# Top-k attention and a SwiGLU block: where the epsilon is added, when the reciprocal runs, and the order of the first loads

## The chip, the core and the metric

The kernel runs on one core of a Trainium2 chip. A core has five engines that run side by side, each with its own instruction queue in program order: TensorE (PE in the profile, with its weight loads as PEld), VectorE (DVE), ScalarE (ACT), GpSimd (POOL) and SyncE (SP), which here only issues DMA transfers. They meet through semaphores. The metric is the device time of the whole kernel in microseconds, the median of several runs.

## What is computed

```python
# q, k, v: (8 batches, 8 heads, 576 rows, 64)
scores = scale * np.matmul(q, k.transpose(0, 1, 3, 2))
kth = np.partition(scores, -top_k, axis=-1)[..., -top_k:-top_k + 1]      # top_k = 32
scores = np.where(scores >= kth, scores, -1000000000.0)
attn = np.exp(scores - np.max(scores, axis=-1, keepdims=True))
attn = attn / (np.sum(attn, axis=-1, keepdims=True) + 1e-09)
x = np.matmul(attn, v)                      # then to (4608 tokens, 512)
g = x @ w_gate                              # (512, 1536)
out = (g * (1.0 / (1.0 + np.exp(-g))) * (x @ w_val)) @ w_out             # (1536, 512)
```

All is float32. The 1e-09 is the epsilon of this document.

## The kernel before

**Units.** Attention is cut into 160 units: for each of 8 batches, five tiles of query rows (four of 128 rows, one of the 64 rows left over), and for each tile four pairs of heads. `units` (line 273) lists them in this order, so units 0 to 19 are batch 0. A unit of a full tile has two heads per instruction pair, one of the last tile has both heads stacked in one (units 16 to 19, 36 to 39 and so on). In the loop over `n` (line 833) the selection of unit `n`, the softmax of unit `n - 1`, the transposes of unit `n - 2` and the product with V of units `n - 4` and `n - 3` stand side by side.

**Selection on VectorE.** `select` (line 318) finds the 32 largest of 576 scores in four rounds: MAX8 finds eight, MATCH_REPLACE8 strikes them out. With two heads this makes seven pairs of instructions: MAX8, MATCH, MAX8, MATCH, MAX8, MATCH, MAX8. The helper `dve(k)` (line 840) emits `k` of these pairs, and after some of them a step of the rounding of the weights (`rounding`), unless it is told `beside=False`.

**Softmax.** `shift` (line 340) puts the bias of the exponential on GpSimd. `weigh` (line 350) runs on ScalarE: a Prelu that masks, then an Exp that also sums its row into `tot`. `normalize` (line 368) adds the epsilon to `tot` and takes the reciprocal, both on VectorE, and after a `yield` multiplies `e` by it: on GpSimd for both heads of units 0 to 11 (line 380), from unit 12 on the first head on ScalarE (line 378) and the second on GpSimd. In the loop the line `run(norm)` (line 890) stands between the fifth pair of the selection (`dve(1)`, line 888) and the last two (`dve(2, beside=False)`, line 891). `turn` (line 384) transposes `e` on TensorE, and ScalarE copies the result out of PSUM.

**Loads and preparation.** `load` (line 215) fetches K and Q of one pair of heads: for K and then for Q, two transfers of the 512 main rows and one of the last 64 rows. All go through SP's queue, except two of pair 0, which ScalarE issues. `prep` (line 250) transposes them on TensorE in three steps, each with a PSUM bank from `ps_t` (5 banks) and copies by ScalarE: K's main rows, the last rows of both, Q's main rows, with a `yield` after the last rows. `fetch` (line 772) starts `prep` three units ahead, its halves at lines 885 and 887.

**Weights.** The three weight matrices are loaded in 36 pieces and rounded by ScalarE (L112 to L115), VectorE (L119) and GpSimd (L120, L121), spread over the first units. A piece's buffer is loaded again when GpSimd is done with it.

**Feed-forward.** Blocks of 256 tokens go through TensorE in pieces (`piece`, line 745) that the loop puts between the attention's steps, by a credit that `share` (line 781) gives per unit. The first two blocks are taken by `feed_half` and `out_half` (L488, L540), the later ones by `feed` (L572, L638).

**Order.** The order within PE, DVE, ACT and POOL is that in which the program emits the instructions: at the end a dependency is added from each instruction to the next of its engine. Only SP's queue is ordered by the scheduler.

Of the kernel before, what the change touches and what calls it, by code (L numbers as in the profile page):

```python
# [10 lines left out]
FP32 = mybir.dt.float32  # L11
# [4 lines left out]
P = 128  # L16
# [3 lines left out]
EPS = 1.0e-9  # L20
# [5 lines left out]
def kernel(  # L26
# [37 lines left out]
    nc = tc.nc  # L64
    B, H, S, D = q.shape
# [3 lines left out]
    R = S - JP  # L69
    NHP = H // 2  # L70
# [2 lines left out]
    MS = MC // 2  # L73
    MQ = MC // 2
    NBLK = B * S // BLK
    scale = 1.0 / float(D) ** 0.5
    assert D == 64 and R == 64 and H * D == DM and DM == 512 and B * S % BLK == 0

# [7 lines left out]
    ps_t = ctx.enter_context(tc.tile_pool(name="ps_t", bufs=5, space=PSUM))  # L86
    ps_f = ctx.enter_context(tc.tile_pool(name="ps_f", bufs=3, space=PSUM))

    ident = consts.tile([P, P], FP32, name="ident")
# [109 lines left out]
    def rounding(n):  # L199
        for _ in range(n):  # L200
            next(weight, None)
# [13 lines left out]
    def load(i):  # L215
        b, hp = pairs[i]
        h = slice(2 * hp, 2 * hp + 2)
        kq = ld.tile([P, 2, J, 2, D], FP32, tag="kq", name="kq_in")
        kq_last = ld.tile([P, 2, D], FP32, tag="kql", name="kq_last")
        for n, src in ((0, k), (1, q)):  # L220
            for hh in range(2):
                queue = nc.scalar if hh == 1 and i == 0 else nc.sync
                queue.dma_start(
                    kq[:, n, :, hh, :],
                    src[b, 2 * hp + hh, 0:JP].rearrange("(p j) d -> p j d", j=J),
                )
            nc.sync.dma_start(
                kq_last[n * R : (n + 1) * R], src[b, h, JP:S].rearrange("h p d -> p h d")
            )
        raw[i] = (kq, kq_last)  # L230
# [19 lines left out]
    def prep(i):  # L250

        kq, kq_last = raw.pop(i)
        slab = slabs.tile([P, R + S + S], FP32, tag="kqT", name="kqT")
        for n, at in ((0, R), (None, S), (1, S + 2 * R)):
            ps = ps_t.tile([P, 512], FP32, tag="t", name="kqps")
            if n is None:
                nc.tensor.transpose(
                    ps[:, 0:P], kq_last[:].rearrange("p h d -> p (h d)"), ident[:]
                )
                nc.scalar.copy(slab[:, at : at + P], ps[:, 0:P])  # L260
                nc.scalar.copy(slab[:, 0:R], ps[:, 0:R])
                yield
                continue
            for c in range(J):
                nc.tensor.transpose(  # L265
                    ps[:, c * P : (c + 1) * P],
                    kq[:, n, c].rearrange("p h d -> p (h d)"),
                    ident[:],
                )
            nc.scalar.copy(slab[:, at : at + JP], ps[:])  # L270
        preps[i] = slab

    units = [(b, qt, hp) for b in range(B) for qt in range(J + 1) for hp in range(NHP)]
# [2 lines left out]
    def n_heads(qt):  # L276

        return 1 if qt == J else 2
# [71 lines left out]
    def weigh(n):  # L350


        st = state[n]
        sc, m, e, heads, bias = st.pop("sc"), st.pop("m"), st["e"], st["heads"], st.pop("bias")
        tot = small.tile([P, 2], FP32, tag="tot", name="tot")
        for t, hs in enumerate(heads):
            nc.scalar.activation(  # L357
                e[:, hs], sc[:, hs], AF.Prelu, bias=m[:, t, TOP_K - 1 : TOP_K], scale=-1.0,
                alpha=SMALL,
            )  # L360
        for t, hs in enumerate(heads):
            nc.scalar.activation(  # L362
                e[:, hs], e[:, hs], AF.Exp, bias=bias[:, t : t + 1], scale=-1.0 / SMALL,
                accum_out=tot[:, t : t + 1],
            )
        st["tot"] = tot

    def normalize(n):
        st = state[n]
        tot, e, heads = st.pop("tot"), st["e"], st.pop("heads")  # L370
        nh = len(heads)
        for t in range(nh):
            nc.vector.tensor_scalar_add(tot[:, t : t + 1], tot[:, t : t + 1], EPS)  # L373
        nc.vector.reciprocal(tot[:, 0:nh], tot[:, 0:nh])  # L374
        yield
        for t, hs in enumerate(heads):
            if t == 0 and n >= 3 * NHP:
                nc.scalar.mul(e[:, hs], e[:, hs], tot[:, t : t + 1])  # L378
            else:
                nc.gpsimd.tensor_tensor(  # L380
                    e[:, hs], e[:, hs], tot[:, t : t + 1].to_broadcast([P, S]), ALU.mult
                )
# [83 lines left out]
    def flush(queue):  # L466
        while queue:
            queue.pop(0)()
# [89 lines left out]
    def feed(kb):  # L558
# [136 lines left out]
        left, right = slice(0, DH), slice(DH, DM)  # L695
        if kb == NBLK - 1:

# [40 lines left out]
    NU = len(units)  # L738
    todo = list(range(1, NBLK))
    current = []  # L740
# [4 lines left out]
    def piece():  # L745

        if len(on_act) > 1:
            flush(on_act)
        if len(on_pool) > 1:
            flush(on_pool)  # L750
        for job in early_jobs[:]:
            cost = next(job, 0)
            if cost == 0:
                early_jobs.remove(job)
            elif cost is not None:
                return cost
        if early_jobs:
            return 0
        while True:
            if not current:  # L760
                if not todo or done.get(todo[0], 0) < NHP * BLK:
                    return 0
                flush(on_act)
                flush(on_pool)
                current.append(feed(todo.pop(0)))
            cost = next(current[0], 0)
            if cost == 0:
                current.pop()
                continue
            return cost  # L770

    def fetch(n):

        b, qt, hp = units[n]
        i = b * NHP + hp
        if qt == 0:
            yield from prep(i)
        if qt == J and i + NHP < len(pairs):
            load(i + NHP)

    def share(n):


        others = 0.0
        costs = [(m, 0.7) for m in scored(n) + valued(n)] + [(n - TURN, 0.6)]
        for m, cost in costs:
            if m >= 0:
                others += cost * (0.5 if units[m][1] == J else 1)
        if units[n + 3][1] == 0:
            others += 0.6  # L790

        beside = 6.1 if n < 8 * NHP else 6.4
        return beside * n_heads(units[n][1]) / 2 - others

    def scored(n):

        ahead = [n + 1] if n < 2 else [] if n % 2 else [n + 1, n + 2]
        return [m for m in ahead if m < NU]

    def valued(n):  # L800

        behind = [] if n % 2 else [n - 4, n - 3]
        return [m for m in behind if 0 <= m < NU]

    def pieces(n):
        for _ in range(n):
            if credit[0] >= 1:
                credit[0] -= piece()

    def run(steps):  # L810
        for _ in steps:
            pass
# [6 lines left out]
                load_v((b + 1) * NHP + hp)  # L819

    load(0)
    rounding(2)
    load(1)
    run(fetch(0))
# [8 lines left out]
    for n in range(NU + 3):  # L833
        nh = n_heads(units[n][1]) if n < NU else 1
        topk = select(n) if n < NU else no
        norm = normalize(n - 1) if 0 <= n - 1 < NU else no
        nxt = [scores(m) for m in scored(n)]
        ahead = fetch(n + 3 if n else 2) if n + 3 < NU else no

        def dve(k, beside=True):  # L840

            for _ in range(k * nh):
                next(topk, None)
                due[0] += 5 / 6 if beside else 0
                if due[0] >= 1:
                    due[0] -= 1
                    rounding(1)

        if n >= NU - NHP:
            credit[0] = 8.0  # L850
        else:
            credit[0] = min(credit[0] + share(n), share(n) + 1)
        flush(on_act)
        if 0 <= n - 1 < NU:
            shift(n - 1)
        flush(on_pool)
        if nxt:
            run(nxt.pop(0))
        if valued(n):
            finish_units(valued(n))  # L860
        if nxt:
            next(nxt[0])
        early[0]()
        if 0 <= n - 1 < NU:
            weigh(n - 1)
        if nxt:
            run(nxt.pop())


        dve(2, beside=False)  # L870
        if n == 0:
            run(ahead)
            load(3)
            ahead = fetch(3)
        if n < NHP:
            load_v(n)
        pieces(2)
        flush(on_act)
        dve(1)
        dve(1)  # L880
        if 0 <= n - TURN < NU:
            run(turn(n - TURN))

        flush(on_pool)
        next(ahead, None)
        pieces(1)
        next(ahead, None)
        dve(1)
        pieces(1)
        run(norm)  # L890
        dve(2, beside=False)
        run(topk)
        pieces(6)
    while piece():
# [49 lines left out]
```

## Time and profile before

| | us |
|---|---|
| Median of 3 runs (lowest, highest) | 1765.2 (1764.88, 1767.09) |
| The profiled execution | 1765.43 |
| Its span, first to last instruction | 1763.6 |
| PE busy | 1679.7 (95% of the span) |
| DVE busy | 1483.0 (84%) |
| ACT busy | 1256.7 (71%) |
| POOL busy | 797.1 (45%) |

The mean granted clock of TensorE was 0.973 of full speed. The DMA engines were busy for 12.4% of the span with the loads and stores of this program, most of it in the first 200 us.

How to read it: "busy" is the time in which an engine executes, over the whole span, and the span has stages of different kinds. A row of the costliest groups reads line, engine, operation, output and inputs by name, shapes, count; then busy time, mean nanoseconds of one, and the idle time of the engine just before these instructions with what ended most of it. The three that this document turns on:

```profile
L373 DVE TENSOR_SCALAR tot<-tot 128x1 f32<-128x1 f32 x288 | 36.6, 145 | 187.6 <-ACT e L362 187.4
L362 ACT ACTIVATE e<-e,bias 128x576 f32<-128x576 f32 x288 | 221.0, 774 | 39.9 <-POOL bias L345 37.1
L378 ACT ACTIVATE e<-e,tot 128x576 f32<-128x576 f32 x148 | 118.5, 800 | 38.3 <-DVE tot L374 38.1
```

The first is the add of the epsilon, one instruction per head: 288 of them, and VectorE stood idle 187.6 us before them over the whole run, nearly all of it until ScalarE's Exp (L362) had ended. The third is ScalarE's multiply by the reciprocal, before which ScalarE waited for VectorE.

In a timeline a row reads start, length, engine, line, operation, and in brackets the idle time before it and what ended it. The chain of waits is the work that ended last, followed back; a row of it is start, length, engine and line.

### The profile page before, as it was taken

How to read it: one execution, taken by the hardware profiler on the slowest of the kernel's cores; microseconds unless marked ns; L12 is line 12 of the kernel's file. 1: busy time of each engine (PE TensorE's matmuls, PEld its weight loads, DVE VectorE, ACT ScalarE, POOL GpSimd, SP SyncE). 2: the span in 40 equal slices, each digit the busy share in tenths (PEclk: the TensorE clock that was granted, in tenths of full speed). 3: DMA queues.
4: the chain of work that ended last, by engine and by line, in shares of the span. 5: the costliest groups of instructions: out<-in, count | busy, mean ns of one | idle time of the engine just before them, and what ended most of it. 6: DMA issues, size and time to landing. Idle time of an engine off the chain costs nothing.

```text
span 1763.6 us, 31788 instructions
## 1 busy us (share of the span) xinstructions
PE 1679.7 (95%) x11396; PEld 1403.7 (80%) x11396; DVE 1483.0 (84%) x3371; ACT 1256.7 (71%) x2869; POOL 797.1 (45%) x910
## 2 busy tenths in 40 slices
PE   4678999899999999999999999999999999999999
PEld 3467688688888788887888878888888888888887
DVE  6999899998898898897989888998988889998300
ACT  7898686678777676777677786777776777676531
POOL 3798544243353524352435324443335343535334
PEclk7688999899999999999999999999999999999999
DMA  7432030003000030002100030000300020000000
GB/s 205 133 112 93 20 78 1 13 1 79 19 13 2 18 79 1 13 1 53 45 13 1 13 71 27 1 13 15 83 1 13 1 56 15 13 1 13 1 13 12
DMA packets 109310, 59.73 MB, mean 34 GB/s; under 512 B 88544, under 2 KB 96992, under 8 KB 109152
## 3 DMA queue, kind: packets, MB, share of 16 engines
q1 hardware_dynamic: 108016, 57.37, 12.4%
q8 instruction: 90, 1.47, 0.3%
q14 instruction: 68, 0.56, 0.1%
q10 hardware_dynamic: 1136, 0.33, 0.1%
HBM read 48.23 MB, written 9.44 MB: 33 GB/s over the span
## 4 chain that ended last, share of the span: by engine, by line
PE 84%; DVE 6%; ACT 6%; POOL 2%; issue 1%; SPq 1%; DMA 0%; ACTq 0%; POOLq 0%
PE f L572 37%; PE av L428 9%; PE x_ps L638 9%; PE s L310 7%; PE y_ps L638 7%; PE etps L394 7%; PE f L488 4%; DVE m L330 3%; DVE e L334 3%; ACT e L362 2%; PE s L296 2%; PE kqps L265 1%; ACT e L357 1%; DVE size L119 1%; ACT sc L315 1%
## 5 line engine op out<-in xcount | busy, mean ns | idle before, releaser
L330 DVE MAX8 m<-e 128x8 f32<-128x576 f32 x864 | 615.5, 749 | 3.3
L334 DVE MATCH_REPLACE8 e<-m,e 128x576 f32<-128x576 f32 x576 | 424.1, 743 | 0.0
L572 PE MATMUL f<-xT,wg 128*128 128x256 f32 x1536 | 354.4, 381 | 0.0
L572 PE MATMUL f<-xT,wv 128*128 128x256 f32 x1536 | 353.1, 380 | 0.0
L572 PEld LDWEIGHTS f<-xT,wg 128*128 128x128 f32 x1536 | 287.5, 190 | 44.7 <-issue 7.9
L572 PEld LDWEIGHTS f<-xT,wv 128*128 128x128 f32 x1536 | 287.1, 190 | 43.4 <-issue 6.8
L608 POOL TENSOR_TENSOR h<-h,half_g 128x512 f32<-128x512 f32 x96 | 122.3, 1274 | 333.6 <-ACT h L607 325.7
L362 ACT ACTIVATE e<-e,bias 128x576 f32<-128x576 f32 x288 | 221.0, 774 | 39.9 <-POOL bias L345 37.1
L394 PE MATMUL etps<-ident,e 128*128 128x128 f32 (+1 forms) x1312 | 182.9, 282 | 45.4 <-ACT sc L315 19.9
L394 PEld LDWEIGHTS etps<-ident,e 128*128 128x128 f32 (+1 forms) x1312 | 155.0, 143 | 74.6 <-POOL e L380 24.5
L357 ACT ACTIVATE e<-sc,m 128x576 f32<-128x576 f32 x288 | 211.1, 784 | 2.6 <-DVE m L330 2.6
L334 DVE MATCH_REPLACE8 e<-m,sc 128x576 f32<-128x576 f32 x288 | 212.0, 743 | 0.0
L330 DVE MAX8 m<-sc 128x8 f32<-128x576 f32 x288 | 203.4, 743 | 9.4 <-ACT sc L315 9.4
L613 POOL TENSOR_TENSOR h<-h,val 128x512 f32<-128x512 f32 x96 | 122.4, 1275 | 194.7 <-ACT val L612 171.0
L315 ACT ACTIVATE sc<-s 128x288 f32<-128x288 f32 x512 | 167.1, 413 | 54.7 <-PE s L310 54.2
L380 POOL TENSOR_TENSOR e<-e,tot 128x576 f32<-128x576 f32 x140 | 160.2, 1148 | 78.5 <-DVE tot L374 70.7
L373 DVE TENSOR_SCALAR tot<-tot 128x1 f32<-128x1 f32 x288 | 36.6, 145 | 187.6 <-ACT e L362 187.4
L395 ACT COPY et<-etps 128x512 f32<-128x512 f32 (+1 forms) x448 | 182.9, 488 | 13.8 <-PE etps L394 13.6
L310 PE MATMUL s<-kqT 64*128 64x288 f32 x1024 | 171.4, 447 | 20.2 <-ACT kqT L270 8.3
L428 PE MATMUL av<-et,v 128*64 128x128 f32 (+1 forms) x2560 | 160.6, 269 | 0.0
L310 PEld LDWEIGHTS s<-kqT 64*128 64x128 f32 x1024 | 94.6, 192 | 66.2 <-issue 23.7
L378 ACT ACTIVATE e<-e,tot 128x576 f32<-128x576 f32 x148 | 118.5, 800 | 38.3 <-DVE tot L374 38.1
(82 smaller groups left out, 2269.7 us busy)
## 6 DMA issues: line engine op xcount, KB each, us to landing
v<-in_v_dram SPq DMA_DIRECT2D x32, 256.0 KB, 3.3
kq_in<-in_k_dram SPq DMA_DIRECT2D x63, 128.0 KB, 2.8
kq_in<-in_q_dram SPq DMA_DIRECT2D x63, 128.0 KB, 3.0
w<-in_moe_w_gate_dram SPq DMA_DIRECT2D x12, 512.0 KB, 3.8
w<-in_moe_w_val_dram SPq DMA_DIRECT2D x12, 512.0 KB, 3.8
w<-in_moe_w_out_dram SPq DMA_DIRECT2D x12, 512.0 KB, 3.5
out_dram<-o SPq DMA_DIRECT2D x38, 128.0 KB, 2.4
out_dram<-o SPq DMA_DIRECT2D x16, 256.0 KB, 2.6
```

Source lines behind the costliest of these rows:

```text
L310: nc.tensor.matmul(ps[:, 0:half], slab[d, q0 : q0 + P], slab[d, k0 : k0 + half])
L315: nc.scalar.mul(sc[:, i * half : (i + 1) * half], ps[:, 0:half], scale)
L330: nc.vector.max(m[:, t, 8 * r : 8 * r + 8], cur[:, hs])
L334: nc.vector.match_replace(e[:, hs], m[:, t, 8 * r : 8 * r + 8], cur[:, hs], LOWEST)
L357: nc.scalar.activation(e[:, hs], sc[:, hs], AF.Prelu, bias=m[:, t, TOP_K - 1 : TOP_K], scale=-1.0, alpha=SMALL,)
L362: nc.scalar.activation(e[:, hs], e[:, hs], AF.Exp, bias=bias[:, t : t + 1], scale=-1.0 / SMALL, accum_out=tot[:, t : t + 1],)
L380: nc.gpsimd.tensor_tensor(e[:, hs], e[:, hs], tot[:, t : t + 1].to_broadcast([P, S]), ALU.mult)
L394: nc.tensor.transpose(ps[0:kl, c * P : (c + 1) * P], e[:, k0 : k0 + kl], ident[:])
L395: nc.scalar.copy(et[0:kl, c0 : c0 + cn, :], ps[0:kl, 0 : cn * P].rearrange("p (c j) -> p c j", c=cn),)
L428: nc.tensor.matmul(av[d, i, 0:ql], weights_, moving, start=c == (0 if last else J), stop=c == (J if last else J - 1),)
L572: nc.tensor.matmul(ps[:, i, :], w[:, kc, m * P : (m + 1) * P], x[:, kc, :], start=(kc == 0), stop=(kc == KC - 1),)
L638: nc.tensor.matmul(ps, lhsT, T[i][m], start=m == 0, stop=m == MQ - 1)
```

## The change

Three things are changed.

- For the first 32 units (`AHEAD`), the epsilon is added by one ScalarE instruction at the end of `weigh`, for both heads at once, instead of by one VectorE instruction per head in `normalize`; and one more pair of the selection is emitted before `run(norm)`, so that the reciprocal stands between the sixth pair and the last. From unit 32 on both are as before.
- `load` issues the main rows of K and Q first and then the last rows of both. `prep` goes K, Q, last rows, with the `yield` after K. This holds for all 32 pairs of heads.
- After the first `load`, TensorE transposes the identity 12 times into a PSUM bank that nobody reads.

```diff
+    AHEAD = 8 * NHP
...
                     src[b, 2 * hp + hh, 0:JP].rearrange("(p j) d -> p j d", j=J),
                 )
+        for n, src in ((0, k), (1, q)):
             nc.sync.dma_start(
                 kq_last[n * R : (n + 1) * R], src[b, h, JP:S].rearrange("h p d -> p h d")
             )
...
-        for n, at in ((0, R), (None, S), (1, S + 2 * R)):
+        for n, at in ((0, R), (1, S + 2 * R), (None, S)):
...
                 nc.scalar.copy(slab[:, 0:R], ps[:, 0:R])
-                yield
                 continue
...
             nc.scalar.copy(slab[:, at : at + JP], ps[:])
+            if n == 0:
+                yield
...
+        if n < AHEAD:
+            nc.scalar.add(tot[:, 0 : len(heads)], tot[:, 0 : len(heads)], EPS)
         st["tot"] = tot
...
-        for t in range(nh):
+        for t in range(nh if n >= AHEAD else 0):
             nc.vector.tensor_scalar_add(tot[:, t : t + 1], tot[:, t : t + 1], EPS)
...
-        beside = 6.1 if n < 8 * NHP else 6.4
+        beside = 6.1 if n < AHEAD else 6.4
...
     load(0)
+    warm = ps_t.tile([P, 512], FP32, tag="t", name="warm")
+    for _ in range(12):
+        nc.tensor.transpose(warm[:, 0:P], ident[:], ident[:])
...
         pieces(1)
+        if n < AHEAD:
+            dve(1, beside=False)
         run(norm)
-        dve(2, beside=False)
+        dve(1 if n < AHEAD else 2, beside=False)
         run(topk)
```

`NHP` is 4, so `AHEAD` is 32, and the line with `beside` keeps its value.

## The prediction

> **What bounds the kernel now.** I read the busy tenths first, then busy time by stage, the chain of waits, the timeline of VectorE (DVE) in the first units, and PE's waits where the stages show PE idle. The stages were cut where the chain changes engine.
>
> ```profile
> PE   4678999899999999999999999999999999999999
> DVE  6999899998898898897989888998988889998300
> ...
> 0.00:77.00 77.00, 37.38 (x172) 24.62 (x172) 62.24 (x142) 59.52 (x131) 43.16 (x45) 0.68 0.63 173
> 77.00:135.00 58.00, 45.53 (x380) 39.89 (x380) 57.83 (x128) 52.91 (x117) 50.76 (x46) 0.85 0.40 119
> 135.00:172.00 37.00, 33.99 (x287) 32.22 (x287) 33.16 (x73) 31.37 (x68) 32.18 (x28) 0.92 0.28 87
> 172.00:306.00 134.00, 132.12 (x1041) 105.43 (x1042) 122.05 (x275) 99.15 (x231) 64.53 (x71) 0.98 0.14 36
> 306.00:334.00 28.00, 19.70 (x147) 14.58 (x146) 27.90 (x68) 18.30 (x45) 9.89 (x13) 0.82 0.05 20
> 334.00:1764.00 1430.00, 1410.99 (x9372) 1187.02 (x9371) 1179.80 (x2690) 995.44 (x2284) 596.62 (x712) 1.00 0.09 22
> ```
>
> The columns after the length are busy us of PE, weight loads, DVE, ACT and POOL, then PE's granted clock. PE runs at about 99% from 172 us on, except 306 to 334 us, where it is idle 8.3 us and DVE is full. The work on PE is the same before and after, so time can only be won where PE is idle: before 77 us, 12.5 us in 77 to 135, 3 us in 135 to 172, and 8.3 us in 306 to 334.
>
> ```profile
> 19.94 4.14 DMA w<-in_moe_w_val_dram
> 24.11 0.66 ACT size L112
> ...
> 33.76 0.15 DVE L373 TENSOR_SCALAR tot<-tot 128x1 f32<-128x1 f32 x1 [2.09 <-ACT e L362]
> 34.51 0.15 DVE L373 TENSOR_SCALAR tot<-tot 128x1 f32<-128x1 f32 x1 [0.60 <-ACT e L362]
> 34.70 0.17 DVE L374 RECIPROCAL tot<-tot 128x2 f32<-128x2 f32 x1
> ...
> 45.09 0.20 DVE L373 TENSOR_SCALAR tot<-tot 128x1 f32<-128x1 f32 x2
> 45.32 0.17 DVE L374 RECIPROCAL tot<-tot 128x2 f32<-128x2 f32 x1
> 45.41 0.07 DVE L334 MATCH_VALUE_LOAD e<-m,e 128x8 f32 x1
> ...
> PE etps L394 <- ACT sc L315: 5.3, 1, 5.3
> PE etps L394 <- POOL e L380: 3.2, 4, 1.2
> ...
> 332.64 0.78 ACT L378 ACTIVATE e<-e,tot 128x576 f32<-128x576 f32 x1 [3.83 <-DVE tot L374]
> ```
>
> The first two lines are the chain: the start hangs on the third weight load's landing at 24.1 us, for which ACT sits idle, and ACT then runs without a gap until the Exp of unit 0 ends at 34.5. The DVE lines show the price of the two adds: first add to reciprocal 0.23 us, reciprocal to the next instruction 0.09. After 34.7 us DVE has no gap until 149 us. The two waits of PE (of 94 to 135 us) end on ACT and POOL, not on DVE.
>
> **What the Trainium skill says.** "ScalarE: Activation LUTs", section "What ACT_TABLE_LOAD costs", gives 186 ns plus 0.833 ns per element for an ACTIVATE with immediate operands, and about 93 ns of overlap with the next. No add of two elements is in this trace; its nearest row, the accumulator read of L362, has a mean of 198 ns and a step of 0.1 us. "VectorE: DVE Perf Modes", section on the TRN2 errata, says that ops with an SBUF source pay a fixed cost per instruction; the trace agrees, one element costs 145 ns on DVE. "TensorE: Matmul & The Clock Gate", Part 1, says that PE falls to half clock after an idle window of about 3.4 us; the trace agrees: 16 matmuls of L488 took 3.62 us after the 5.3 us wait, 1.95 us later. "DMA: Bandwidth & Descriptors", section "Issuing engines are not separate DMA queues", has all loads on the same 16 engines; here SP issues one load per 0.65 us without a pause to 20 us.
>
> **Part 1, K and Q first, and the transposes of the identity.** In the built order SP's first four loads become K, Q, last K, last Q; every load of all 32 pairs is still there, and the first V load (three of its four issues) moves ahead of pair 2's K and Q, which come 3 x 0.65 = 2 us later. The third weight load is the 29th issue of SP in both orders, so it still lands near 24.1 us. PE in before waited 0.66 us for the last rows, and Q's transposes, copy and the first scores came behind them. With Q first, scores can start about 1.2 us sooner (8.0 to 6.8), and PE at full clock takes perhaps 0.5 us off the transposes and scores. The 12 extra transposes, at the 0.24 us step of the first four, take about 3 us between 1.3 (identity ready) and K at 4.3, so they delay K by 0 to 0.5 us. Unit 0 on DVE may start 1 to 2 us earlier than 10.77. I count none of it: ACT then waits for the same weight load, and DVE waited 2.09 + 0.60 us at 33.8 for ACT's Exp. Without that cover the part is worth 1 to 2 us; if pair 2's late loads cost up to 1.6 us, the same wait hides them. In later batches the order only swaps a bank of PSUM; the 32 preparations could each move by 0.1 us either way, together perhaps 1 us: I take 0.
>
> **Part 2, reciprocal one pair later.** At each place where DVE is the path and waits for the Exp, a pair of two MATCH_REPLACE8 (1.46 us) now runs before the reciprocal instead of after. At 34.7 us the reciprocal itself stays (Exp ends 34.5, ACT's add ends about 0.2 later), and only a MAX8 pair of 1.33 us follows: unit 2 starts at 36.2 instead of 37.56, 1.38 us gained. The same wait at 164 us (1.99 + 0.61) is not on PE's way: PE's 3 us wait there ends on POOL at 171 us, and POOL came from ACT. The one at 302 us (0.25 + 0.60) leads to the stage where DVE is full: 1.4 us gained at unit 27. The later reciprocal costs 1.46 - 0.23 = 1.23 us where someone waits for it. In the first 11 units nobody does: POOL takes the product up 2.7 us or more after the reciprocal from unit 1 on. At 332 us ACT does (3.83 us), and PE's scores stand behind ACT: there 1.23 is given back.
>
> **Part 3, the adds.** DVE loses two adds, 0.23 us per unit of two heads. Units 2 to 6, where DVE leads all engines: 5 x 0.23 = 1.15. Units 26 to 28: 3 x 0.23 = 0.69, of which the first is part of the wait above, so 2 x 0.23 = 0.46. In units 11 to 25 DVE is not the bound: nothing. ACT gains one add per unit behind the Exp, waiting on the accumulator read; behind it are queued score copies and weight rounding, and PE waits for the PSUM banks. Bounds per add: 0.1 us (step of the accumulator read) to 0.26 (the accumulator read's overlap of 0.1 lost, the single time of 0.19 less 0.09 of overlap with the next, and some 0.06 for the wait); I take 0.19, the skill's single time. They count where ACT is gapless and on PE's way: units 7, 8, 9 (112 to 135 us) 0.57; unit 11 0.19; units 17 and 18 (ACT chain at 221 to 229 us) 0.38.
>
> **Sum.** Lead when PE becomes the bound: 1.38 + 1.15 - 0.57 = 1.96 at 135 us. To 306 us: -0.19 - 0.38 = 1.39. Through 306 to 334: 1.4 + 0.46 - 1.23 = +0.63. In all 2.0 us. The profiled execution took 1765.43 us (span 1763.6 and 1.8 around it): 1763.4. The median of the runs is 0.2 lower: 1765.2 - 2.0 = 1763.1, 0.12% less. About 0.2%, 3.5 us, is what a measurement of this kernel can tell from no change.
>
> **Rivals.**
> - More of it arrives. The chain as printed runs on DVE in 164 to 184 us too; then the 1.38 and a unit's 0.23 count there as well: 2.0 + 1.6 = 3.6. If a shorter wait also spares PE one window at half clock (3.4 us at half speed, 1.7 lost), it is 5.3: 1759.9. For it: PE's clock is 0.85 in 77 to 135. Against: PE's waits there end on ACT and POOL, which do no less.
> - Nothing arrives: ACT, gapless from 112 to 140 us, takes 0.26 per add from unit 2 on, and POOL's backlog (50.76 of 58 us) does not move up: 1765.
> - Slower: ACT stands in order behind its multiply L378. From unit 26 to 30 the multiply starts 0.1 to 0.2 us after the reciprocal, so ACT waits for it already. If DVE has won nothing there, each such unit costs PE up to 1.23 us: 5 x 1.23 = 6.2, less the lead of 1.4: +4.8, 1770. It decides from three such units on (3.7 against 2.0 gained). Against: after 334 us PE has no idle time to those waits.
>
> **How the numbers follow.** Forecast 0.50 (own range 1761 to 1765), more of it 0.30, nothing 0.07, slower 0.13. Faster by over 0.2% is the second case and a quarter of the first: 0.43. Same: 0.37 + 0.07 = 0.44. Slower 0.13. The range takes the forecast, most of the second case and the unknown 1 to 2 us of the start: 1758.5 to 1766.5.
>
> **What would show it.** Unit 2's first MAX8 at 36.2 us; no gap before the reciprocal in units 2 to 10; units of 9.7 us instead of 9.95 where DVE is full (27 to 31); reciprocal of unit 28 about 0.6 us ahead of PE's shift. Wrong if the third weight load lands earlier or later than 24 us by more than 0.5, if ACT's wait before L378 grows in units 13 to 24, or if PE's half-clock stretches at 110 to 121 and 134 to 141 us change in number.

## The result, and the profile after

| | before | after |
|---|---|---|
| Median (lowest, highest; runs) | 1765.47 us (1763.58, 1767.44; 19) | 1763.04 us (1759.75, 1764.23; 19) |
| The profiled execution, its span | 1765.43, 1763.6 | 1760.46, 1758.7 |

The medians are 2.4 us apart and the means 3.5. The ratio is that of the means, 0.998, with a 95% interval of 0.9973 to 0.9987: 3.5 us less, 2.3 to 4.8. The two measures differ because the runs of after lie in two groups, nine from 1759.8 to 1762.0 and ten from 1763.0 to 1764.2 us, and the median is the lowest of the upper group. The profiled execution of after is itself 2.6 us below its median, so 4.9 us separate the two profiles. That gap has to be kept in mind with every profile below.

The page of after, busy time and busy tenths:

```profile
PE 1680.1 (96%) x11408; PEld 1404.4 (80%) x11408; DVE 1475.0 (84%) x3311; ACT 1263.0 (72%) x2901; POOL 798.2 (45%) x910
...
PE   5678999899999999999999999999999999999999
...
DVE  6998898998898898898989888998988888998300
...
L378 DVE TENSOR_SCALAR tot<-tot 128x1 f32<-128x1 f32 x228 | 29.7, 147 | 170.4 <-ACT e L365 170.0
```

The change did what it says: 60 of the 288 adds have left VectorE, whose busy time fell by 8.0 us, and ScalarE's rose by 6.3. Three of the stages, cut as before (length, busy us of PE, weight loads, DVE, ACT and POOL, PE's granted clock):

```profile
77.00:135.00 58.00, 45.17 (x387) 39.57 (x384) 58.00 (x120) 54.43 (x123) 51.85 (x47) 0.88 0.40 119
...
306.00:334.00 28.00, 22.04 (x158) 16.78 (x157) 28.00 (x61) 20.32 (x52) 8.25 (x12) 0.82 0.05 19
334.00:1764.00 1430.00, 1407.17 (x9359) 1184.60 (x9357) 1175.27 (x2676) 993.66 (x2280) 597.06 (x711) 1.00 0.09 22
```

PE's idle time from 306 to 334 us fell from 8.3 to 6.0 us. In 77 to 135 us VectorE is full as before, only its work is further along. Counts shift across the borders, since all work is earlier; the last stage ends 4.9 us sooner.

How far each kernel is ahead is read better from an event that both have: for VectorE the first MAX8 of each unit, for TensorE the start of the same matmul. The timeline of before, and then of after, at the start and in the stage from 306 us:

```profile
10.77 1.42 DVE L330 MAX8 m<-sc 128x8 f32<-128x576 f32 x2 [9.35 <-ACT sc L315]
...
18.91 0.43 DVE L119 TENSOR_SCALAR size<-size 128x512 int32<-128x512 int32 x1 [1.50 <-ACT size L112]
...
22.70 1.40 DVE L330 MAX8 m<-sc 128x8 f32<-128x576 f32 x2
...
37.56 1.41 DVE L330 MAX8 m<-sc 128x8 f32<-128x576 f32 x2
...
323.52 2.18 PE L394 MATMUL etps<-ident,e 128*128 128x128 f32 x9 [3.32 <-ACT e L378]
```

```profile
24.42 0.67 ACT L113 ACTIVATE size<-w 128x512 f32<-128x512 f32 x1 [4.23 <-DMA w<-in_moe_w_val_dram]
...
8.69 1.42 DVE L333 MAX8 m<-sc 128x8 f32<-128x576 f32 x2 [7.27 <-ACT sc L318]
...
19.11 0.43 DVE L120 TENSOR_SCALAR size<-size 128x512 int32<-128x512 int32 x1 [3.78 <-ACT size L113]
...
22.90 1.40 DVE L333 MAX8 m<-sc 128x8 f32<-128x576 f32 x2
...
34.59 0.21 ACT L365 ACTIVATION_READ_ACCUMULATOR e<-e,bias 128x1 f32 x1
34.83 0.20 ACT L370 ACTIVATE tot<-tot 128x2 f32<-128x2 f32 x1
34.94 0.65 ACT L113 ACTIVATE size<-w 128x512 f32<-128x512 f32 x1
...
35.07 0.17 DVE L379 RECIPROCAL tot<-tot 128x2 f32<-128x2 f32 x1 [1.73 <-ACT tot L370]
...
36.47 0.75 DVE L333 MAX8 m<-sc 128x8 f32<-128x576 f32 x1
...
320.90 2.18 PE L399 MATMUL etps<-ident,e 128*128 128x128 f32 x9 [2.11 <-ACT e L383]
```

Unit 0 starts at 8.69 us instead of 10.77, yet unit 1 starts at 22.90 instead of 22.70: VectorE stood 3.78 us at 19.11 us for ScalarE's step of the second weight piece, where it had stood 1.50, and the earlier start is lost there. Then ScalarE stood 4.23 us for the third weight load. Unit 2 starts at 36.47 instead of 37.56. From there the lead grows by 0.25 us in each unit: 1.09 at unit 2, 2.36 at unit 7. At 320.90 PE waits 2.11 us for ScalarE's multiply, where it waited 3.32 before. From 340 to 800 us TensorE is 2.8 to 3.1 us ahead. The last 1.8 came at 820 us, where the profile of before has a stretch in which TensorE was granted half its clock, and this one has none.

### The profile page after: what moved, and what is told of

Its sections match the earlier page's. It is cut to its first block, busy times and chain, and to the rows that moved or that the text cites. A ratio compares the mean times of both kernels' runs of the same rounds, so it can differ in the third digit from the quotient of the medians.

```text
span 1758.7 us, 31764 instructions
## 1 busy us (share of the span) xinstructions
PE 1680.1 (96%) x11408; PEld 1404.4 (80%) x11408; DVE 1475.0 (84%) x3311; ACT 1263.0 (72%) x2901; POOL 798.2 (45%) x910
## 4 chain that ended last, share of the span: by engine, by line
PE 84%; DVE 8%; ACT 5%; POOL 1%; issue 1%; DMA 1%; SPq 0%; ACTq 0%; POOLq 0%
PE f L577 38%; PE x_ps L643 9%; PE av L433 9%; PE y_ps L643 7%; PE s L313 7%; PE etps L399 7%; DVE m L333 4%; DVE e L337 3%; PE f L493 3%; PE s L299 2%; ACT e L365 1%; PE kqps L266 1%; DVE size L120 1%; ACT e L360 1%; PE o_ps L545 0%
## 5 line engine op out<-in xcount | busy, mean ns | idle before, releaser
L318 ACT ACTIVATE sc<-s 128x288 f32<-128x288 f32 x512 | 167.3, 414 | 52.9 <-PE s L313 52.4
L400 ACT COPY et<-etps 128x512 f32<-128x512 f32 (+1 forms) x448 | 183.5, 490 | 13.9 <-PE etps L399 13.7
L378 DVE TENSOR_SCALAR tot<-tot 128x1 f32<-128x1 f32 x228 | 29.7, 147 | 170.4 <-ACT e L365 170.0
L383 ACT ACTIVATE e<-e,tot 128x576 f32<-128x576 f32 x148 | 118.8, 803 | 35.5 <-DVE tot L379 35.2
```

Of the source, the lines that this page charges most:

```text
L318: nc.scalar.mul(sc[:, i * half : (i + 1) * half], ps[:, 0:half], scale)
L400: nc.scalar.copy(et[0:kl, c0 : c0 + cn, :], ps[0:kl, 0 : cn * P].rearrange("p (c j) -> p c j", c=cn),)
```

## The experiments

All medians and ratios stand against the kernel before in the same comparison. "Lead" is by how much unit 7 starts earlier on VectorE than in the profile of before, one profiled execution each. Some 0.3 us of it is the execution's own: in the nine profiles that leave the third weight load where it was, ScalarE's step that waits for it began between 23.78 and 24.42 us. The parts were taken singly first.

| kernel | lead, us | median, us (runs) | before, us | ratio (95% interval) |
|---|---|---|---|---|
| start_only | -0.07 | 1764.61 (13) | 1765.2 | 0.9999 (0.9991 to 1.0007) |
| eps_only | 1.00 | 1763.51 (21) | 1765.2 | 0.9991 (0.9985 to 0.9998) |
| recip_only | 1.81 | 1763.82 (13) | 1765.2 | 0.9993 (0.9984 to 1.0001) |
| eps_recip_only | 2.81 | 1762.82 (21) | 1765.2 | 0.9985 (0.9979 to 0.9992) |
| ahead7 | 2.56 | 1762.38 (20) | 1765.18 | 0.9985 (0.9978 to 0.9991) |
| w2_early | 4.02 | 1759.62 (7) | 1765.18 | 0.9972 (0.9962 to 0.9983) |
| w2_early_again | 4.06 | 1759.91 (5) | 1766.07 | 0.9964 (0.9951 to 0.9976) |
| w2_early_oldstart | 4.17 | 1761.49 (10) | 1765.18 | 0.9978 (0.9969 to 0.9988) |
| no_cover | 6.11 | 1757.93 (5) | 1766.07 | 0.9952 (0.9939 to 0.9966) |
| no_cover_oldstart | 4.87 | 1760.00 (5) | 1766.07 | 0.9967 (0.9955 to 0.998) |
| ahead_all | 2.77 | 1771.03 (5) | 1765.18 | 1.0033 (1.002 to 1.0045) |
| all_eps | 2.80 | 1770.79 (8) | 1766.07 | 1.003 (1.002 to 1.004) |

### The parts of the change

**start_only**: the new order of loads and preparation, and the transposes of the identity; the adds and the reciprocal as before.

```diff
-        if n < AHEAD:
-            nc.scalar.add(tot[:, 0 : len(heads)], tot[:, 0 : len(heads)], EPS)
...
-        for t in range(nh if n >= AHEAD else 0):
+        for t in range(nh):
...
-        if n < AHEAD:
-            dve(1, beside=False)
         run(norm)
-        dve(1 if n < AHEAD else 2, beside=False)
+        dve(2, beside=False)
```

> The loads, the order of the preparation and the 12 transposes of the identity alone; the epsilon and the reciprocal as before. My theory (the start is hidden behind the third weight load and the Exp of unit 0): unit 0 starts near 8.7 us instead of 10.8, unit 2 at 37.6 to 37.9 as before, and the time is that of before within 0.5 us. Rival (a start 2 us sooner is part of the gain): unit 2 is 0.5 us or more ahead of before and the time 0.5 to 2 us lower.

No difference can be measured: the interval is 1.6 us less to 1.2 more. It alone would not exclude the rival; the timeline on VectorE does:

```profile
8.85 1.42 DVE L333 MAX8 m<-sc 128x8 f32<-128x576 f32 x2 [7.43 <-ACT sc L318]
...
22.63 1.40 DVE L333 MAX8 m<-sc 128x8 f32<-128x576 f32 x2
...
37.64 1.41 DVE L333 MAX8 m<-sc 128x8 f32<-128x576 f32 x2
```

1.92 us won at unit 0 are gone at unit 1, and unit 2 starts where it did (37.64 against 37.56).

**eps_recip_only**: the two other parts, with the start of before.

```diff
-        for n, src in ((0, k), (1, q)):
             nc.sync.dma_start(
                 kq_last[n * R : (n + 1) * R], src[b, h, JP:S].rearrange("h p d -> p h d")
             )
...
-        for n, at in ((0, R), (1, S + 2 * R), (None, S)):
+        for n, at in ((0, R), (None, S), (1, S + 2 * R)):
...
-    for _ in range(12):
-        nc.tensor.transpose(warm[:, 0:P], ident[:], ident[:])
```

> The epsilon on ScalarE and the later reciprocal for the first 32 units alone; the start as before. My theory: unit 2 leads before by 1.1 to 1.4 us, unit 7 by 2.3 to 2.6, unit 35 by 2 to 3, and the time is 2 to 3 us lower: all of the change. Rival: without the sooner start only half of it, 1 to 1.3 us.

The gain is here, as far as can be told: 2.7 us by the ratio (1.4 to 3.7), beside 3.5 (2.3 to 4.8) for after, and 2.4 by both pairs of medians. The leads were larger than expected, 1.55 us at unit 2, 2.81 at unit 7 and 4.02 at unit 35. At unit 2, 0.15 us of this is the third weight load, for which ScalarE's step began at 23.96 us and not at 24.11; the later lead is that of a profiled execution 1.4 us below its median.

**eps_only** and **recip_only** are eps_recip_only without the later reciprocal, and without the adds on ScalarE.

> The epsilon on ScalarE for the first 32 units, the reciprocal at its old place, the start as before. My theory: the wait for the Exp in unit 1 stays and is lengthened by ScalarE's add, so unit 2 is 0.3 us late; each unit up to 7 then wins 0.23 to 0.25, so unit 7 leads by about 0.9; adds on ScalarE take most of that, and the time is within 1 us of before. Rival (the adds off VectorE are the gain): 2 us lower. Rival (ScalarE's adds cost 0.26 each wherever it is gapless): 1 us or more higher.

> The reciprocal one pair later for the first 32 units, the two adds still on VectorE, the start as before. My theory: unit 2 leads by 1.46 us (one MATCH pair), unit 7 by the same 1.46, and nothing is won per unit; at 306 to 334 us the later reciprocal gives back what the shorter wait wins, so the time is 1.2 to 1.6 us lower. Rival (ScalarE's multiply waits longer from unit 12 on): the lead is gone by unit 35, the time as before or higher.

```profile
34.95 0.17 DVE L377 RECIPROCAL tot<-tot 128x2 f32<-128x2 f32 x1 [3.29 <-ACT tot L368]
...
37.81 1.40 DVE L331 MAX8 m<-sc 128x8 f32<-128x576 f32 x2
...
48.18 1.40 DVE L331 MAX8 m<-sc 128x8 f32<-128x576 f32 x2
```

This is VectorE in eps_only. Unit 2 is 0.25 us later than before. 0.19 of it is the third weight load (ScalarE's step began at 24.30 us and not at 24.11), and 0.06 is left for the reciprocal that now waits for ScalarE's add, where 0.3 was expected. From then on the lead grows by 0.25 us per unit, and unit 3 starts where it did. The time fell by 1.7 us: the expectation "within 1 us" was too low, and the rival's 2 us was nearer, though the interval (0.3 to 2.6 us) holds both. In the same view of recip_only:

```profile
34.37 0.17 DVE L375 RECIPROCAL tot<-tot 128x2 f32<-128x2 f32 x1
...
35.77 1.40 DVE L331 MAX8 m<-sc 128x8 f32<-128x576 f32 x2
...
46.39 1.40 DVE L331 MAX8 m<-sc 128x8 f32<-128x576 f32 x2
```

The 1.8 us come all at once, at unit 2, and stay to unit 12. 1.46 were expected, and 1.46 it is when the weight load is taken out (ScalarE's step began at 23.78 us, 0.33 sooner than in before). The time fell by 1.4 us, but the interval just includes no change. The rival with ScalarE's multiply has little for it here: the lead at unit 35 is 2.60 us and not gone. Added up, the medians of the two parts give 3.1 us and together they gave 2.4: the same within the intervals.

**ahead7**: `AHEAD = 7` in after, `share` as it was.

> As the kernel after, but with the epsilon on ScalarE and the later reciprocal in units 0 to 6 alone (TensorE's share per unit as in before). Theory 'the lead is made where VectorE runs without a pause, units 2 to 6, and is only carried from there': VectorE leads before by about 2.4 us at unit 7, as after does, and by 2.0 to 2.6 at unit 35; time within 0.5 us of after, 1762.5 to 1763.6. Theory 'it is earned over all 32 units, 0.25 us in each': the part up to unit 7 is about half of it, so 1764.0 to 1764.6.

1762.38 is 0.1 us beyond the lower end of the first expectation and 1.6 below the second. Against its own before the ratio gives 2.7 us less (1.6 to 3.9), where after has 3.5 (2.3 to 4.8). What the adds and the later reciprocal do in units 7 to 31 brings, on balance, nothing that can be told from the runs. One number missed: in its profile the lead at unit 35 was 0.87 and not 2.0 to 2.6. That profiled execution took 1764.21 us, 1.8 above its median, which is about what the lead is short of.

### The cover of the start

**w2_early**: the third piece of the weights is issued right after the loads of pair 1.

```diff
         lags = (5, 2, 0)
+        hoist[0] = lambda: upto(2, 1)
...
     load(1)
+    hoist[0]()
     run(fetch(0))
```

> As the kernel after, with one load moved: the third piece of the weights is issued right after the K and Q of pair 1 instead of behind the loads of pairs 2 and 3, so that ScalarE's wait of 4.23 us for it at 24.4 us goes. Theory 'that wait hides the earlier start': VectorE's waits of 0.36 and 1.73 us in unit 1 go, unit 2 leads before by 3.0 to 3.4 us instead of 1.1, and 1 to 2 us of it arrive: 1761 to 1762. Rival 'the fourth piece or VectorE's order then holds unit 1': unit 2 within 0.5 us of after's and the time within 0.6 us of it.

> w2_early once more, beside no_cover on the same chip. Theory 'the load covers about 2 us': 1759 to 1761.5. Rival 'the first result was luck of few runs': 1762 to 1763.5, as after.

Two results, 5.6 and 6.2 us below before by the medians and 4.9 and 6.4 by the ratios, where after is 2.4 and 3.5 below. So the moved load brought between 1.4 and 3.7 us; that it is more than the 1 to 2 expected is not shown, and the intervals meet that of after. The lead at unit 2 was 2.75 us, less than the 3.0 to 3.4 expected. The timeline (its lines are three further down in the code, L336 is the MAX8):

```profile
25.48 0.67 ACT L113 ACTIVATE size<-w 128x512 f32<-128x512 f32 x1 [2.17 <-DMA w<-in_moe_w_val_dram]
...
19.29 0.43 DVE L120 TENSOR_SCALAR size<-size 128x512 int32<-128x512 int32 x1 [4.00 <-ACT size L113]
...
33.42 0.15 DVE L382 RECIPROCAL tot<-tot 128x2 f32<-128x2 f32 x1
...
34.81 1.40 DVE L336 MAX8 m<-sc 128x8 f32<-128x576 f32 x2
```

The wait of 4.23 us is gone, the next one (2.17 us, for the fourth piece) is half as long, and VectorE no longer stands before the first reciprocal: unit 2 starts at 34.81, 1.66 us before that of after. But unit 1 did not move (23.07): VectorE still stood 4.00 us at 19.29 for ScalarE's step of the second piece.

**w2_early_oldstart**: the same moved load with the start of before.

> The same moved load as in w2_early, but with the start of before (Q last, no transposes of the identity): epsilon on ScalarE and later reciprocal are kept. Theory 'the early start counts once the load no longer covers it': 0.5 to 2 us slower than w2_early, unit 2 later than there by about that. Rival 'the start is hidden behind the K and Q of pair 1 too': unit 2 within 0.3 us of w2_early's and the times within 0.6 us.

Unit 2 starts at 34.64 us, within 0.2 of w2_early's, as the rival had it. The median is 1.9 us higher, as the theory had it, but the intervals overlap. This pair leaves it open.

**no_cover**: that wait of 4.00 us is taken away too. It ended so late because ScalarE did the K and Q copies of pair 2 first, and stood for their transposes. The second piece's step now goes ahead of them, and the fourth piece is issued ahead of the loads of pair 3.

```diff
+    hoist[0](1, 1)
+    hoist[0](2, 1)
     run(fetch(0))
...
     load(2)
+    hoist[0](3, 1)
...
         if n == 0:
+            hoist[0](1, 1)
+            hoist[0](1, 2)
             run(ahead)
```

Here `hoist[0](i, k)` is `upto(i, k)` of the weights: piece `i`, counted from 0, up to its step `k`, the load being step 1 and ScalarE's part step 2.

> As w2_early, and two more covers of the early start taken away: ScalarE takes its step of the second weight piece (VectorE stands 4.00 us for it at 19.29 us in w2_early) ahead of the K and Q copies of pair 2, and the fourth piece is issued ahead of the loads of pair 3 (ScalarE waits 2.17 us for it at 25.48 us in w2_early). Theory 'each wait goes and the next one is shorter': unit 1 starts near 19.7 us instead of 23.1, unit 2 near 32 us instead of 34.8, and the time is 1757 to 1759. Rival 'the lead is spent before TensorE sees it': unit 2 earlier, but the time within 0.6 us of w2_early.

```profile
16.58 0.42 DVE L120 TENSOR_SCALAR size<-size 128x512 int32<-128x512 int32 x1
...
20.36 1.40 DVE L336 MAX8 m<-sc 128x8 f32<-128x576 f32 x2
...
31.30 0.17 DVE L382 RECIPROCAL tot<-tot 128x2 f32<-128x2 f32 x1 [0.51 <-ACT tot L373]
...
32.70 1.41 DVE L336 MAX8 m<-sc 128x8 f32<-128x576 f32 x2
```

Unit 1 starts at 20.36 us (19.7 expected), unit 2 at 32.70 (32 expected). The time is 1757.93, 8.1 us below before: the lowest median of the study, and faster than after, whose interval (0.9973 to 0.9987) does not meet this one's (0.9939 to 0.9966). That it is faster than w2_early is not shown: those intervals meet.

**no_cover_oldstart**: the same with the start of before.

> As no_cover, with the start of before (Q last, no transposes of the identity). Theory 'with the covers gone the early start is worth something': unit 1 1.0 to 1.8 us later than in no_cover, unit 2 0.5 to 1.5 us later, and 0.5 to 1.5 us slower. Rival 'the start is hidden at unit 1 whatever is done': unit 2 within 0.3 us of no_cover's.

```profile
17.37 1.49 DVE L120 TENSOR_SCALAR size<-size 128x512 int32<-128x512 int32 x1 [0.21 <-ACT size L113]
...
22.23 1.40 DVE L334 MAX8 m<-sc 128x8 f32<-128x576 f32 x2
...
33.95 0.74 DVE L334 MAX8 m<-sc 128x8 f32<-128x576 f32 x1
```

Unit 1 starts 1.87 us later than in no_cover, unit 2 1.25 us later, and the median is 2.1 us higher, a little over the 0.5 to 1.5 expected, with intervals that overlap. This fits the theory, but it does not show that VectorE now keeps the early start. Unit 0 began only 0.49 us later here (10.51 against 10.02). Another 1.07 of the 1.87 us is VectorE's step of the second weight piece (L120), which took 1.49 us instead of 0.42: it began while GpSimd's L122 was running and ended 0.29 us after that had ended, at 18.57. It came there because ScalarE's step of the piece began at 16.66 us and not at 14.94, and up to then TensorE, whose matmuls ScalarE waited for, had been at half clock, where in no_cover it was at full clock from 10.7 to 17.6 us. Such a stretch comes with the old start too (11.3 to 14.8 us in before), so the clock of these two executions explains the difference as well as the start does.

Moving the weight pieces, on the other hand, does not need the new start: with the old one the time is 6.1 us below before. What it would bring without the adds and the later reciprocal was not tried.

### Further than 32 units

**ahead_all**: `AHEAD` is all 160 units. **all_eps**: the epsilon on ScalarE in all 160, the later reciprocal in the first 32 alone.

```diff
+    ADDED = 40 * NHP
...
-        if n < AHEAD:
+        if n < ADDED:
             nc.scalar.add(tot[:, 0 : len(heads)], tot[:, 0 : len(heads)], EPS)
...
-        for t in range(nh if n >= AHEAD else 0):
+        for t in range(nh if n >= ADDED else 0):
```

> As the kernel after, but with the epsilon on ScalarE and the later reciprocal in all 160 units. Theory 'from 334 us on TensorE sets the pace and VectorE's slack takes both': within 0.5 us of after, 1762.5 to 1763.6, with VectorE about 8 us less busy per 32 units and TensorE's busy time unchanged. Rival 'ScalarE's queue': the later reciprocal holds the multiply and what is queued behind it on ScalarE, score copies for TensorE among it, so TensorE waits in units after 32 and the time is over 1766.

> As after, with the epsilon on ScalarE in all 160 units, but the later reciprocal in the first 32 alone. Theory 'in ahead_all it was the later reciprocal that made TensorE wait, for multiply and transposes come after it': within 1 us of after, 1762 to 1764, and no half-clock stretches at the batch changes near 611, 820 and 1028 us. Rival 'the add in ScalarE's queue does it': 1766 to 1771, with the stretches.

Both were slower than before by 5 to 6 us, and nearly the same. So my theories fell twice: VectorE's slack after 334 us does not make the move free, and the add alone, without the later reciprocal, is enough to cost this. PE's timeline around 610 us, where one batch ends and the next begins, in after and then in all_eps:

```profile
610.78 0.33 PE L259 MATMUL kqps<-ident,kq_last 128*128 128x128 f32 x1 [2.00 <-ACT et L400]
...
612.42 1.04 PE L433 MATMUL av<-et,v 128*64 128x128 f32 x16
...
616.96 0.30 PE L399 MATMUL etps<-ident,e 128*64 128x128 f32 x1 [0.64 <-ACT sc L318]
```

```profile
611.08 0.33 PE L260 MATMUL kqps<-ident,kq_last 128*128 128x128 f32 x1 [2.24 <-ACT et L401]
...
613.30 1.92 PE L434 MATMUL av<-et,v 128*64 128x128 f32 x16
...
1442.58 0.30 PE L400 MATMUL etps<-ident,e 128*64 128x128 f32 x1 [0.88 <-ACT sc L319]
```

PE's waits end on ScalarE copies (L400 and L318 in after, L401 and L319 in all_eps), which in all_eps stand behind the add in ScalarE's queue. 2.00 became 2.24, and 0.64 at 616 and at 1435 us became 0.89 and 0.88: 0.24 to 0.25 us per add. From 340 to 1690 us PE has twelve waits of 0.48 to 2.00 us in after, 11.0 us together. In all_eps eleven of them are longer by about 0.24, and five new ones of 0.12 to 0.26 stand beside them, 14.7 in all. That is 3.8 of the 7.2 us (medians) or 8.8 us (ratios) by which all_eps and after differ, each against its own before. For the rest the profiles offer half clock: after the longer wait the 16 matmuls at 613.30 took 1.92 us for 1.04. At the three batch changes near 611, 820 and 1028 us, all_eps had two such stretches and ahead_all three, while each of the twelve other profiles had one at most. A stretch costs about 1.6 us there (worked out in the last section). How many the median runs had is not known, so the rest of the difference stays open.

## Why the prediction was right

1763.1 was forecast, and the median is 1763.04. That this is so close is luck. The prediction's own sum, 1765.2 less 2.0, is 1763.2; the median stands at the edge between two groups of runs; and by the ratio the gain is 3.5 us, 2.3 to 4.8, which is more than the 2.0 forecast. What held is the direction, the range and, at each place where the traces allow a test, the mechanism. By its steps:

**Part 1, counted at nothing: right, but the reason given was only one of three.** Unit 0 started 2.08 us sooner in the profile of after (1 to 2 estimated), but this depends on the clock that TensorE was granted: from 8.5 to 10.2 us in the eight profiles with the new start, 10.3 to 11.0 in the six with the old one. The third weight load ended ScalarE's wait at 24.42 (24.1 foreseen), and start_only moved nothing. What the prediction did not see is that the start is lost earlier, in VectorE's wait for the second weight piece at 19.11 us, and that the fourth piece stands behind the third. "Without that cover the part is worth 1 to 2 us" was therefore too simple: with the load moved, unit 2 came at 34.81 us with the new start and at 34.64 with the old one (w2_early, w2_early_oldstart). With all three waits gone the two differ, but not clearly by the start. For the later batches, taken at 0, the traces show a small effect. PE's waits at the batch changes near 611, 820 and 1028 us are 2.00, 1.52 and 1.51 us in after and 2.32, 1.84 and 1.84 in before, and the same in every other profile with the same order and no added ScalarE work there; from 340 to 1600 us TensorE's lead grows by 0.4 us in the six such profiles (in two of them after a spared stretch at half clock is taken out), and by less than 0.1 with the old order. start_only does not show it in time.

**Part 2: right, in mechanism and size.** 1.38 us was taken at unit 2, and 1.09 came in after, 1.55 in eps_recip_only. The difference is the third weight load, which is the execution's own: ScalarE's step began at 24.11 us in before, 24.42 in after and 23.96 in eps_recip_only. From that step to unit 2 it is 13.45 us in before and 12.05 in both others, 1.40 less. In recip_only, where no add on ScalarE stands before the reciprocal, it is 1.46 less.

**Part 3: 0.25 us per unit and not 0.23.** The units without a wait are 9.70 us long instead of 9.95, and the lead from unit 2 to unit 7 is 1.27 for a forecast of 1.15. ScalarE's add costs 0.24 and not 0.19: the upper of the two bounds, 0.26, was nearly right. Between 210 and 230 us, where two adds (units 17 and 18) were put down at 0.38, TensorE's lead falls by 0.48 in eps_recip_only and 0.47 in eps_only, and by nothing in recip_only. The trace says why. In before the next instruction began before the accumulator read was over (a step of 0.1 us for 0.2 long); the add waits for that read, begins 0.03 us after its end, and the next instruction begins 0.11 later. In the Trainium skill, "ScalarE: Activation LUTs", section "What ACT_TABLE_LOAD costs", the 186 ns and the overlap of 93 ns fit the add itself, 0.20 us with a step of 0.11; what has to be added is the overlap that the instruction before it loses.

**From 135 to 306 us: not testable.** The sum has a lead of 1.96 us at 135 us and 1.39 at 306. In after TensorE's lead was 1.51 and 2.15. It rose between them because before has 13.6 us at half clock from 134 to 179 us and after 10.2 from 131 to 176. In start_only, which has no lead to begin with, it rises by 3.7 us from 135 to 190 us in the same way.

**The stage from 306 to 334 us: right, 0.63 forecast and 0.71 came.** TensorE's lead rose from 2.15 us at 306 to 2.86 at 340 us in after, and from 3.29 to 4.02 in eps_recip_only. The terms can be read off. At unit 27 VectorE leads by 3.56 us, 1.4 more than TensorE, and this is the 1.4 of the later reciprocal. The reciprocal itself stands later in its unit and leads by 2.31 at unit 26 (310.17 for 312.48), 1.25 less: the 1.23 given back. From there each unit adds 0.25, and the reciprocal of unit 28 leads by 2.80. In recip_only the first two cancel: TensorE's lead is 4.23 at 306 and 4.24 at 325 us. So what the stage gives comes from the adds. PE's wait for the multiply shrank by more, 1.21 us (3.32 to 2.11), because TensorE's lead had first fallen to 1.65 us at 315 us; it falls there by 0.5 in eps_only and eps_recip_only too, and not in recip_only.

**The rivals.** "Nothing arrives" is out: the interval excludes 1. "Slower, behind ScalarE's multiply" did not come; before the multiply ScalarE has waited 35.5 us in all in after and 38.3 in before. The same engine and the same in-order queue, but behind the add instead of the multiply and after unit 32, is what made ahead_all and all_eps slower. "More arrives" is not out: its 3.6 us lie inside the interval, beside the ratio's 3.5, and a spared stretch at half clock (at 820 us) is part of what the profiled execution of after won. How often that happens the profiles can't say, one for each kernel.

**Signs named beforehand.** No gap before the reciprocal in units 2 to 10: so it was. Units of 9.7 us: so it was. The reciprocal of unit 28 led by 2.80 us where TensorE had entered the stage with 2.15, so by 0.65 more, for 0.6. The third weight load was within 0.5 us of 24. ScalarE's wait before the multiply in units 13 to 24 did not grow (0.63 us in before, 0.11 in after). The stretches at half clock did change in number, 10.2 us at 110 to 121 becoming 6.8. But they changed in start_only too (6.8 there, at 111.9), which has no lead: this sign was no test.

## What to carry to other kernels

Before counting on an early start, list every wait between it and the bound: here three stood in a row, and with none or one of them taken away the third unit did not feel the start. Whether it does with all three gone is open. Taking the three away by moving weight pieces in two queues brought the change from 2.4 to 8.1 us, and 6.1 of it came with the old start. A tiny instruction that waits for its own engine's last result costs its length and the lost overlap, 0.24 us here; it belongs on the engine that has a gap at that place, which is ScalarE in the first seven units and VectorE from unit 32 on.

Read a difference between two kernels from events that both have, and take out what belongs to the execution (here when a load landed, and where the half-clock stretches lay) before calling a term too large or too small.

## What the runs showed of the hardware

The stretches at half clock lie on a grid of about 3.4 us whose place differs from execution to execution: their lengths are whole multiples of 3.41 us (3.4, 6.8 and 10.2 most often) wherever the end of the span does not cut one off, and around unit 9 they began between 106 and 112 us in different profiles. The Trainium skill, "TensorE: Matmul & The Clock Gate", Part 1, says that the window runs freely and so its phase at the start varies; these traces agree.

One stretch among the matmuls after 340 us costs about 1.6 us: TensorE's lead in recip_only over before, 2.60 us, became 4.22 where before has a stretch at 820 us, and 2.60 again where recip_only has its own at 1023 us. That is one reason why two profiles can lie further apart than the medians of their kernels. The clock also decides when unit 0 begins: in w2_early the first scores took 1.52 us after the 12 transposes and unit 0 began at 8.65 us, while in w2_early_again, the same kernel, PE was still at half clock, they took 2.57 us, and unit 0 began at 10.13.

VectorE's rounding step (L119 in before, L120 elsewhere) takes 0.40 to 0.44 us, but 0.99 to 1.49 in thirteen cases in the first 80 us of before, after, no_cover and no_cover_oldstart. Each of the thirteen began while a step of GpSimd was running and ended 0.28 to 0.29 us after that step had ended.
